# A token-routing kernel: a third copy of the expert slots, whose last slot is 160 columns wide

## The chip, the cores and the metric

The kernel runs on one core of one Trainium2 chip. The metric is device time in microseconds (us): the median of several executions. A profile of one more execution gives the times of single instructions. Engines are called PE (TensorE, matrix multiply), PEld (its weight loads), DVE (VectorE), ACT (ScalarE), POOL (GpSimd) and SP (SyncE, which issues DMAs).

## The reference, cut to what matters

Three stages follow each other: a linear attention over 4 x 768 positions, a mixture of eight experts in which each of the 3072 tokens goes to one expert, and a dense max-out layer.

```python
def _moe_ref(x, modality_id, w_gate, modality_bias, w1, w2):   # x: 3072 x 384
    logits = x @ w_gate + modality_bias[modality_id]           # 8 experts
    e_idx = np.argmax(logits, axis=1)
    ...
    for e in range(E):
        mask = e_idx == e
        h = np.maximum(x[mask] @ w1[e], 0.0)                   # 384 -> 1024
        out[mask] = gate_w[mask, None] * (h @ w2[e])           # 1024 -> 384

def _moe2_ref(x, w1, w2, w3, w_out):
    h = np.maximum(np.maximum(x @ w1, x @ w2), x @ w3)
    return (h @ w_out)
```

How many tokens an expert gets depends on the data. Computed with this reference on its inputs, experts 4, 5 and 6 get 149, 1354 and 1569 tokens and the other five get none.

## The kernel before

The attention runs over 24 tiles of 128 positions. When 16 of them are done, the kernel picks the expert that leads so far (expert 6) and begins to load its weights. The expert stage is cut into slots. A slot gathers the tokens of one expert, at most as many as it has columns, transposes them (`turn`), and runs eight steps `f` over the 1024 hidden features. A step does nine matmuls of the first layer (`first`, L940, three chunks of 128 inputs times three hi/lo products in fp32r, a rounded 4-byte type that the profile prints as f32) and, one step behind, nine of the second layer (`second`, L952). So a slot is 144 matmuls, each with a weight load of 128 columns. ACT and DVE take the hidden values out (`hid`, L943 and L944).

The first three slots are 256 columns wide and all belong to the leading expert. For the rest the kernel chooses one of nine widths, 256 to 384 in steps of 16, on the chip: `Routing.counting` counts the tokens of each expert, works out how many slots each width needs (`per`, `num`), prices them (`cost`) and writes the index of the choice to `sel`. Its work is a chain of small DVE instructions, spread over the steps of slot 0 as a Python generator: `during(f)` asks for the next piece at each step from f = 2 on, so each `yield` puts the rest one step later. The pieces follow the `hid` of their step on DVE. What is left at the end of slot 0 is then issued, and right behind it all five engines load `sel` into a register:

```python
for _ in tally:
    pass
moe.tail = (0, SLOT, still)
chosen = moe.value(route.sel, every, 2 * NW - 1)
```

Only then do slots 1 and 2 follow, with `Routing.placing`, which works out the table of slots (`tab`) on DVE. Behind slot 2 every engine jumps, by the register `chosen`, into one of 18 straight copies of the remaining slots: for each width one that has exactly as many slots as are sure for it, and one that asks after each further slot whether it is there. With the counts above, expert 6 has 801 tokens left after 768, expert 5 has 1354 and expert 4 has 149. At 272 columns that is 3 + 5 + 1 = 9 slots, the cheapest by `cost` and just the sure number, so the exact copy of width 272 runs, slots 3 to 11. Slot 11 is the one slot of expert 4; it takes 272 columns for its 149 tokens. Into these slots the conversion of the max-out weights (L1046 to L1065, on DVE, POOL and SP) and the last part of the routing (`finals`, L552 on PE) are mixed as side jobs. After slot 11 `leave` copies its result to `yt`, and the max-out stage (L1132 and L1157) follows.

Of the kernel before, what the change touches and what calls it, by code (L numbers as in the profile page):

```python
# [16 lines left out]
ALU = mybir.AluOpType  # L17
AX = mybir.AxisListType
# [5 lines left out]
P = 128  # L24
# [4 lines left out]
E = 8  # L29
SLOT = 256  # L30
WIDTHS = tuple(range(SLOT, SLOT + P + 1, P // 8))
NW = len(WIDTHS)
WIDE = WIDTHS[-1]
NJW = (NT - SLOT) // SLOT + 1
OWN = WIDE // P
AHEAD = 3


def last_slot(w):
    return AHEAD + (NT - SLOT - E) // w + E  # L40


def sure_slots(w):
    return AHEAD - (-(NT - AHEAD * SLOT) // w)
# [337 lines left out]
class Routing:  # L382
    def __init__(self, tc, const, ps):
# [18 lines left out]
        self.wsure = const.tile([P, NW], F32, name="wsure")  # L402
        self.wj = const.tile([P, NW, NJW], F32, name="wj")
        self.jj = const.tile([P, NJW], F32, name="jj")
        self.off = const.tile([P, 1, E], F32, name="off")
# [13 lines left out]
    def setup(self):  # L419
# [18 lines left out]
        for i, w in enumerate(WIDTHS):  # L438
            nc.gpsimd.memset(self.wsure[:, i:i + 1], float(sure_slots(w) - AHEAD))
        nc.gpsimd.iota(self.jj, [[1, NJW]], base=0, channel_multiplier=0, **io)  # L440
        yield
        nc.gpsimd.tensor_tensor(self.wj, self.wv.unsqueeze(2).to_broadcast([P, NW, NJW]),
                                self.jj.unsqueeze(1).to_broadcast([P, NW, NJW]), op=ALU.mult)
        yield
# [160 lines left out]
    def counting(self, wk):  # L605
        nc, V = self.nc, self.nc.vector
        tile = lambda shape, nm, dt=F32: wk.tile(shape, dt, tag=f"rt_{nm}", name=f"rt_{nm}")
        some = tile([P, 1, E], "all", BF16)
        self.tally(NTILE, some)
        cps = self.bank("cps")  # L610
        yield
        cnt = self.counts(wk, NTILE, some, cps)
        row = cnt.rearrange("p e o -> p o e")
        rem = tile([P, 1, E], "rem")
        V.tensor_tensor(rem, row, self.off, op=ALU.subtract)
        key = tile([P, 1, E], "key")
        V.scalar_tensor_tensor(key, row, float(E), self.prio, op0=ALU.mult, op1=ALU.add)
        over = tile([P, NW, E, NJW], "over", F16)
        for i in range(NW):
            V.tensor_tensor(over[:, i], rem[:, 0, :].unsqueeze(2).to_broadcast([P, E, NJW]),  # L620
                            self.wj[:, i:i + 1, :].to_broadcast([P, E, NJW]), op=ALU.is_gt)
            if i in (2, NW - 1):
                yield
        per = tile([P, NW, E], "per")
        V.tensor_reduce(per, over, axis=AX.X, op=ALU.add)
        num = tile([P, NW], "num")
        V.tensor_reduce(num, per, axis=AX.X, op=ALU.add)
        cost = tile([P, NW], "cost")
        V.tensor_tensor(cost, num, self.wcost, op=ALU.mult)
        yield  # L630
        V.tensor_tensor(cost, cost, self.wsel, op=ALU.add)
        least = tile([P, 1], "least")
        V.tensor_reduce(least, cost, axis=AX.X, op=ALU.min)
        pick = tile([P, NW], "pick")
        V.tensor_scalar(pick, cost, least, None, op0=ALU.is_equal)
        V.tensor_tensor(num, num, self.wsure, op=ALU.is_gt)
        V.scalar_tensor_tensor(num, self.wsel, 2.0, num, op0=ALU.mult, op1=ALU.add)
        V.tensor_tensor(num, num, pick, op=ALU.mult)
        V.tensor_reduce(least, num, axis=AX.X, op=ALU.add)
        V.tensor_copy(self.sel, least[0:1])  # L640
        self.plan = row, key, per, pick
        yield
# [169 lines left out]
class Experts:  # L812
# [5 lines left out]
    def open(self, st):  # L818
        tc = self.tc
        pool = st.enter_context(tc.tile_pool(name="mx", bufs=1))  # L820
        self.xg = [[pool.tile([P, DM], F32, name=f"xg{i}_{a}") for a in range(2)] for i in range(2)]
        self.xh, self.xl = ([pool.tile([P, KC, WIDE], F32R, name=f"{q}0")] for q in ("xh", "xl"))
        self.raw = (pool.tile([P, KC, FF], F32, name="raw1"), pool.tile([P, KF, DM], F32, name="raw2"))
        self.w = {nm: pool.tile(shape, F32R, name=f"w_{nm}")
                  for nm, shape in (("h1", [P, KC, FF]), ("l1", [P, KC, FF]), ("h2", [P, KF, DM]), ("l2", [P, KF, DM]))}
        self.hid = pool.tile([P, 4 * WIDE], F32R, name="hid")

# [47 lines left out]

    def gather(self, k, n=WIDE):
        for a in range(-(-n // P)):
            self.fetch(k, a, self.rt.gidx[:, OWN * k:OWN * (k + 1)])
# [31 lines left out]
    def open_more(self, pool):  # L910
        for i in range(2):
            self.xg[i] += [pool.tile([P, DM], F32, name=f"xg{i}_{a}") for a in range(2, OWN)]
        self.xh.append(pool.tile([P, KC, WIDE], F32R, name="xh1"))
        self.xl.append(pool.tile([P, KC, WIDE], F32R, name="xl1"))

# [79 lines left out]
        if job is not None:  # L995
            job(f)

    def slot(self, k, n, stop, total, side=()):
        r = self.regs(k, stop)
        sure = sure_slots(n)  # L1000

        def when(i, what):
            if i < min(sure, stop):
                what()
            elif i < stop:
                with self.tc.If(total > i):
                    what()

        cum = [len(side) * c // 18 for c in (0, 3, 6, 9, 12, 15, 17, 18, 18)]
        for f in range(KF):  # L1010
            if f == KF - 1:
                when(k + 1, lambda: self.turn(k + 1, n))
            self.step(k, f, n, r)
            if f == 0:
                when(k + 2, lambda: self.gather(k + 2, n))
            for j in side[cum[f]:cum[f + 1]]:
                j()
        self.tail = (k, n, r)
# [178 lines left out]
def build(tc, aps):  # L1197
    nc = tc.nc
    ET = mybir.EngineType
    with ExitStack() as st:  # L1200
# [4 lines left out]
        with tc.manual_schedule(), ExitStack() as right, ExitStack() as left:  # L1205
            att = Attention(tc, aps, const, ps, dram, x_dram)
            moe = Experts(tc, aps, att.ident, ps, x_dram)
# [4 lines left out]
            route = moe.rt = Routing(tc, const, ps)  # L1212
            mo = MaxOut(tc, aps, route, ps)
            side = route.setup()
            every = (ET.PE, ET.Activation, ET.DVE, ET.Pool, ET.SP)
# [8 lines left out]
            for s in range(NTILE):  # L1224
                att.step(s, hook)
                if s == EARLY + 1:
                    for _ in side:
                        pass
                    side = route.opening(rw, att.logits, att.bias, EARLY, lambda: moe.load_all(
                        moe.value(route.toptab[:, 0:1], (ET.SP,), E - 1)))  # L1230
# [47 lines left out]
            for _ in tally:  # L1278
                pass
            moe.tail = (0, SLOT, still)  # L1280
            chosen = moe.value(route.sel, every, 2 * NW - 1)
            ahead = lambda: tc.switch_hint({e: chosen for e in every}, 2 * NW, "width")
            with tc.If(moe.many > 0) as both:
                places = route.placing(rw)
                for k in range(1, AHEAD):
# [18 lines left out]
            total = moe.tab(0, NSLOT, every, NSLOT)  # L1304
# [7 lines left out]
            conv = mo.converters(left.enter_context(tc.tile_pool(name="m2tmp", bufs=1, reuse_waits="tile")))  # L1312
            jobs, finals = route.landing(mo.land, att.logits)

            for i in tc.Switch({e: chosen for e in every}, 2 * NW, "width"):
                n, exact = WIDTHS[i // 2], i % 2 == 0
                sure = sure_slots(n)
                stop = sure if exact else last_slot(n)
                moe.tail = (AHEAD - 1, SLOT, moe.regs(AHEAD - 1, stop))
                for k in range(AHEAD, sure):  # L1320
                    a, b = (len(conv) * q // (sure - AHEAD) for q in (k - AHEAD, k - AHEAD + 1))
                    c, d = (len(jobs) * q // (sure - AHEAD - 1) for q in (k - AHEAD, k - AHEAD + 1))
                    side = conv[a:b]
                    for q, j in enumerate(jobs[c:d]):
                        side.insert(7 * q + 3, j)
                    if k == sure - 1:
                        for q, j in enumerate(finals):
                            side.insert(3 * q + 1, j)
                    moe.slot(k, n, stop, total, side)
                if exact:  # L1330
                    moe.end()
                    continue

                def more(k):
                    if k == stop:
                        moe.end()
                        return
                    tail = moe.tail
                    with tc.If(total > k) as going:
                        moe.slot(k, n, stop, total)  # L1340
                        more(k + 1)
                    moe.tail = tail
                    with going.Else():
                        moe.end()

                more(sure)
# [55 lines left out]
```

## Time and profile before

| | |
|---|---|
| median of 3 runs | 711.36 us (710.59 to 713.24) |
| the profiled execution | 713.69 us, its span from the first to the last instruction 712.0 us |
| granted TensorE clock, mean | 0.969 of full speed |
| busy PE | 672.2 us, 94% of the span |
| busy DVE, ACT, POOL | 409.7, 230.3, 238.9 us |

The profiled execution took 2.3 us longer than the median. Its stages: the attention up to about 152 us, slots 0 to 2 up to 214 us, slots 3 to 11 from 216 to 402 us, the max-out layer from there on. A start-to-start distance of two matmuls, read off the timeline, is the pace of PE; the busy time of one matmul is longer, because matmuls are pipelined.

### The profile page before, as it was taken

How to read it: one execution, taken by the hardware profiler on the slowest of the kernel's cores; microseconds unless marked ns; L12 is line 12 of the kernel's file. 1: busy time of each engine (PE TensorE's matmuls, PEld its weight loads, DVE VectorE, ACT ScalarE, POOL GpSimd, SP SyncE). 2: the span in 40 equal slices, each digit the busy share in tenths (PEclk: the TensorE clock that was granted, in tenths of full speed). 3: DMA queues.
4: the chain of work that ended last, by engine and by line, in shares of the span. 5: the costliest groups of instructions: out<-in, count | busy, mean ns of one | idle time of the engine just before them, and what ended most of it. 6: DMA issues, size and time to landing. Idle time of an engine off the chain costs nothing.

```text
span 712.0 us, 13675 instructions
## 1 busy us (share of the span) xinstructions
PE 672.2 (94%) x5007; PEld 607.6 (85%) x5007; DVE 409.7 (58%) x849; ACT 230.3 (32%) x545; POOL 238.9 (34%) x257
## 2 busy tenths in 40 slices
PE   7998979898998998999999899999999999999995
PEld 4887868788998998999989788888888888888884
DVE  6999988838845788878787755322322322222321
ACT  3755754552221244222243334111111211211211
POOL 6877764255032338532255201030210220210202
PEclk8999997889999999999999999999999999999999
DMA  8987865620023471322731000010000100100101
GB/s 229 307 244 235 258 203 176 209 73 24 1 62 109 126 223 54 113 85 72 209 105 46 4 0 1 0 45 1 30 15 1 44 1 1 44 1 1 44 1 45
DMA packets 36251, 61.32 MB, mean 86 GB/s; under 512 B 4880, under 2 KB 24976, under 8 KB 36160
## 3 DMA queue, kind: packets, MB, share of 16 engines
q1 hardware_dynamic: 32512, 49.02, 22.9%
q0 software_dynamic: 3648, 11.21, 5.1%
q8 instruction: 42, 0.69, 0.4%
q14 instruction: 49, 0.40, 0.2%
HBM read 50.77 MB, written 9.44 MB: 85 GB/s over the span
## 4 chain that ended last, share of the span: by engine, by line
PE 43%; issue 11%; DVE 2%; POOL 1%; ACT 0%; POOLq 0%; DVEq 0%; ACTq 0%
PE l L1132 24%; PE o L1157 7%; PE acc L952 6%; PE h L940 6%; POOL out_dram L1168 1%; PE inv_out L552 1%; DVE hid L944 0%; PE t L889 0%; DVE m2wo L1062 0%; DVE m2wl L1096 0%; DVE m2raw L1058 0%; POOL x2l L1119 0%; DVE m2wo L1054 0%; PE acc L889 0%; POOLq L1398 0%
## 5 line engine op out<-in xcount | busy, mean ns | idle before, releaser
L1136 DVE TENSOR_TENSOR tm<-tm,l 128x512 f32<-128x512 f32 x72 | 49.4, 687 | 174.2 <-PE l L1132 174.2
L952 PE MATMUL acc<-hid,w_h 128*128 128x272 f32 (+1 forms) x576 | 125.3, 291 | 6.1 <-DVE hid L944 5.6
L1132 PE MATMUL l<-x2h,m2wh 128*128 128x512 f32 x324 | 126.2, 390 | 1.8 <-ACT m2wh L1100 1.8
L1132 PE MATMUL l<-x2h,m2wl 128*128 128x512 f32 x324 | 127.3, 394 | 0.5 <-DVE m2wl L1096 0.5
L1132 PE MATMUL l<-x2l,m2wh 128*128 128x512 f32 x324 | 127.3, 394 | 0.0
L952 PEld LDWEIGHTS acc<-hid,w_h 128*128 128x128 f32 x576 | 96.8, 190 | 8.7 <-DVE hid L944 8.2
L940 PE MATMUL h<-xh,w_h 128*128 128x272 f32 (+1 forms) x288 | 85.2, 296 | 2.8 <-ACTq L1305 1.9
L943 ACT ACTIVATE hid<-h 128x272 fp32r<-128x272 f32 (+1 forms) x96 | 37.8, 394 | 147.5 <-PE h L940 141.1
L940 PE MATMUL h<-xl,w_h 128*128 128x272 f32 (+1 forms) x288 | 83.0, 288 | 0.5 <-DVE xl L892 0.5
L940 PE MATMUL h<-xh,w_l 128*128 128x272 f32 (+1 forms) x288 | 83.1, 289 | 0.3 <-POOL w_l L865 0.3
L952 PE MATMUL acc<-hid,w_l 128*128 128x272 f32 (+1 forms) x288 | 83.0, 288 | 0.0
L1168 POOL DMA_INDIRECT out_dram<-o,row x24 | 23.6, 984 | 160.0 <-ACT o L1165 154.5
L1132 PEld LDWEIGHTS l<-x2h,m2wl 128*128 128x128 f32 x324 | 61.2, 189 | 13.7 <-DVE m2wl L1096 0.9
L1132 PEld LDWEIGHTS l<-x2h,m2wh 128*128 128x128 f32 x324 | 61.0, 188 | 13.8 <-ACT m2wh L1100 2.0
L1132 PEld LDWEIGHTS l<-x2l,m2wh 128*128 128x128 f32 x324 | 61.2, 189 | 12.5 <-DVE x2l L1096 0.5
L1139 ACT CAST hh<-tm 128x512 fp32r<-128x512 f32 x36 | 22.4, 622 | 149.3 <-DVE tm L1136 149.3
L944 DVE SCALAR_TENSOR_TENSOR hid<-h,hid 128x272 fp32r<-128x272 f32 (+1 forms) x96 | 41.5, 432 | 45.0 <-ACT hid L943 40.5
L223 ACT ACTIVATE A<-ident,dot 128x128 f32<-128x128 f32 x192 | 58.7, 391 | 6.9 <-DVE dot L217 6.7
L940 PEld LDWEIGHTS h<-xh,w_h 128*128 128x128 f32 x288 | 55.0, 191 | 3.4 <-issue 3.1
L940 PEld LDWEIGHTS h<-xl,w_h 128*128 128x128 f32 x288 | 54.9, 191 | 0.9 <-DVE xl L892 0.9
L940 PEld LDWEIGHTS h<-xh,w_l 128*128 128x128 f32 x288 | 54.7, 190 | 0.7 <-POOL w_l L865 0.5
L952 PEld LDWEIGHTS acc<-hid,w_l 128*128 128x128 f32 x288 | 54.9, 191 | 0.0
(272 smaller groups left out, 1213.2 us busy)
## 6 DMA issues: line engine op xcount, KB each, us to landing
raw<-in_moe_w_dram SPq DMA_DIRECT2D x24, 384.0 KB, 4.3
m2raw<-in_moe_w_dram SPq DMA_DIRECT2D x18, 384.0 KB, 3.2
kT<-in_kT_dram SPq DMA_DIRECT2D x24, 224.0 KB, 4.1
rT<-in_rT_dram SPq DMA_DIRECT2D x24, 224.0 KB, 4.3
kn<-in_kn_dram SPq DMA_DIRECT2D x24, 192.0 KB, 4.2
rn<-in_rn_dram SPq DMA_DIRECT2D x24, 192.0 KB, 4.5
vn<-in_vn_dram SPq DMA_DIRECT2D x24, 192.0 KB, 4.5
x_rows<-x SPq DMA_DIRECT2D x24, 192.0 KB, 2.7
```

The costliest lines, as they stand in the source:

```text
L223: nc.scalar.mul(t["A"][:, h % 2, h // 2, :], self.ident, t["dot"][:, h:h + 1])
L552: self.nc.tensor.matmul(inv, lhsT=self.lo[:, i, :], rhs=hi[:, :, i], start=(i == 0), stop=(i == n - 1), skip_group_check=True)
L940: nc.tensor.matmul(ps, lhsT=s[w][:, c, fs], rhs=x[:, c, :], start=(i == 0), stop=(i == 3 * KC - 1))
L943: nc.scalar.activation(hh, ps, AF.Relu)
L944: nc.vector.scalar_tensor_tensor(hl, ps, 0.0, hh.bitcast(F32), op0=ALU.max, op1=ALU.subtract)
L952: nc.tensor.matmul(self.bank[c][:, 0:n], lhsT=s[w][:, f, v], rhs=x, start=(f == 0 and q == 0), stop=(f == KF - 1 and q == 2), skip_group_c ...
L1132: nc.tensor.matmul(ps, lhsT=w[:, m, c, fs], rhs=x[:, c, :], start=(n == 0), stop=(n == 3 * KC - 1))
L1136: nc.vector.tensor_tensor(t, t, ps, op=ALU.max)
L1139: nc.scalar.copy(hh, t)
L1157: self.nc.tensor.matmul(self.acc[a], lhsT=x[:, v], rhs=w[:, f, :], start=(f == 0 and q == 0), stop=(f == NF - 1 and q == 2))
L1168: nc.gpsimd.indirect_dma_start(out=self.out[n], out_offset=bass.IndirectOffsetOnAxis(ap=self.rt.row[:, n:n + 1].bitcast(U32), axis=0), in_ ...
```

## The change

`counting` gets a block of fourteen more DVE instructions in place of one. They find the expert that comes last in order, and how many tokens its last slot will hold at each width; where that is at most NARROW = 160, the index is that of a new kind of copy. There are now 27 copies, three for each width. The new kind is the exact one, with a last slot of 160 columns: its transposes (`after`), its matmuls, the hidden values and `leave` have 160 columns, while its gather stays as wide as before. In `counting` a `yield` is added in the middle of the new block.

```diff
+NARROW = SLOT // 2 + 32
...
         V.tensor_scalar(pick, cost, least, None, op0=ALU.is_equal)
         V.tensor_tensor(num, num, self.wsure, op=ALU.is_gt)
-        V.scalar_tensor_tensor(num, self.wsel, 2.0, num, op0=ALU.mult, op1=ALU.add)
+        lk, lm = tile([P, 1, E], "lk"), tile([P, 1], "lm")
+        V.tensor_scalar(lk, rem, 0.0, 1e9, op0=ALU.is_le, op1=ALU.mult)
+        V.tensor_tensor(lk, lk, key, op=ALU.add)
+        V.tensor_reduce(lm, lk, axis=AX.XY, op=ALU.min)
+        V.tensor_scalar(lk, lk, lm, None, op0=ALU.is_equal)
+        yield
+        pl = tile([P, NW, E], "pl")
+        V.tensor_tensor(pl, per, lk.to_broadcast([P, NW, E]), op=ALU.mult)
+        fill = tile([P, NW], "fill")
+        V.tensor_reduce(fill, pl, axis=AX.X, op=ALU.add)
+        V.tensor_scalar(fill, fill, -1.0, None, op0=ALU.add)
+        V.tensor_tensor(fill, fill, self.wv, op=ALU.mult)
+        V.tensor_tensor(lk, lk, rem, op=ALU.mult)
+        V.tensor_reduce(lm, lk, axis=AX.XY, op=ALU.add)
+        V.tensor_scalar(lm, lm, float(NARROW), None, op0=ALU.subtract)
+        V.tensor_scalar(fill, fill, lm, None, op0=ALU.is_lt)
+        V.scalar_tensor_tensor(num, num, 2.0, fill, op0=ALU.mult, op1=ALU.max)
+        V.scalar_tensor_tensor(num, self.wsel, 3.0, num, op0=ALU.mult, op1=ALU.add)
         V.tensor_tensor(num, num, pick, op=ALU.mult)
         V.tensor_reduce(least, num, axis=AX.X, op=ALU.add)
         V.tensor_copy(self.sel, least[0:1])
...
-    def slot(self, k, n, stop, total, side=()):
+    def slot(self, k, n, stop, total, side=(), after=None, sure=0):
         r = self.regs(k, stop)
-        sure = sure_slots(n)
+        after = after or n
...
-                when(k + 1, lambda: self.turn(k + 1, n))
+                when(k + 1, lambda: self.turn(k + 1, after))
...
-            chosen = moe.value(route.sel, every, 2 * NW - 1)
-            ahead = lambda: tc.switch_hint({e: chosen for e in every}, 2 * NW, "width")
+            chosen = moe.value(route.sel, every, 3 * NW - 1)
+            ahead = lambda: tc.switch_hint({e: chosen for e in every}, 3 * NW, "width")
...
-            for i in tc.Switch({e: chosen for e in every}, 2 * NW, "width"):
-                n, exact = WIDTHS[i // 2], i % 2 == 0
+            for i in tc.Switch({e: chosen for e in every}, 3 * NW, "width"):
+                n, exact, last = WIDTHS[i // 3], i % 3 < 2, NARROW if i % 3 == 0 else WIDTHS[i // 3]
...
-                    moe.slot(k, n, stop, total, side)
+                    moe.slot(k, n if k < sure - 1 else last, stop, total, side, last if k == sure - 2 else n, sure)
```

## Rows read from the trace of the kernel before

**Rows 1.** Part 1 of the page: busy us, share of the span, instructions.

```profile
PE 672.2 (94%) x5007; PEld 607.6 (85%) x5007; DVE 409.7 (58%) x849; ACT 230.3 (32%) x545; POOL 238.9 (34%) x257
```

**Rows 2.** Groups by line and shape: count, busy us, mean ns, idle before.

```profile
L940 PE MATMUL h<-xh,w_h 128*128 128x272 f32 x216 | 64.0, 296 | 1.9 <-ACTq L1305 1.9
```

**Rows 3.** PE's timeline, start and duration in us: each pair bounds equal matmuls.

```profile
203.84 0.28 PE L940 MATMUL h<-xh,w_h 128*128 128x256 f32 x1
...
206.00 0.28 PE L940 MATMUL h<-xh,w_h 128*128 128x256 f32 x1
...
310.74 0.29 PE L940 MATMUL h<-xh,w_h 128*128 128x272 f32 x1
...
313.00 0.29 PE L940 MATMUL h<-xh,w_h 128*128 128x272 f32 x1
...
699.99 0.34 PE L1157 MATMUL o<-m2oh,hh 128*128 128x384 f32 x1
...
703.46 0.34 PE L1157 MATMUL o<-m2oh,hl 128*128 128x384 f32 x1
```

**Rows 4.** Single lines: ns minimum, median, maximum; first and last start.

```profile
L952 PEld LDWEIGHTS acc<-hid,w_l x288: 187/188/335, 154.7 to 401.3; 128*128 128x128 f32 x144
...
L248 PEld LDWEIGHTS xps<-A,vn x304: 118/136/231, 41.2 to 150.3; 128*48 128x48 f32 x133, 128*64 128x64 f32 x19
...
L889 PEld LDWEIGHTS t<-ident,xg x72: 137/141/231, 146.8 to 375.1; 128*128 128x128 f32 x72
L889 PE MATMUL t<-ident,xg x72: 270/273/477, 146.8 to 375.2; 128*128 128x128 f32 x72
```

**Rows 5.** PE's timeline: plain f32 matmuls of 120 and transposes of 128 columns.

```profile
82.66 0.50 PE L267 MATMUL xnps<-turn,xT 112*128 112x120 f32 x3
...
83.33 0.28 PE L267 MATMUL xnps<-turn,xT 112*128 112x120 f32 x1
...
210.32 0.82 PE L889 MATMUL t<-ident,xg 128*128 128x128 f32 x6
```

**Rows 6.** DVE's timeline in step 6 of slot 0.

```profile
170.62 0.41 DVE L944 SCALAR_TENSOR_TENSOR hid<-h,hid 128x256 fp32r<-128x256 f32 x1
170.95 0.16 DVE L631 TENSOR_TENSOR rt_cost<-rt_cost,wsel 128x9 f32<-128x9 f32 x1
...
172.29 0.14 DVE L640 CAST sel<-rt_least 1x1 int32<-1x1 f32 x1
172.36 0.40 DVE L944 SCALAR_TENSOR_TENSOR hid<-h,hid 128x256 fp32r<-128x256 f32 x1
```

**Rows 7.** Instructions on the tile `sel`: PE's sequencer loads it.

```profile
L832 PEldq TENSOR_LOAD <-sel x1: 311/311/311, 172.5 to 172.5; - x1
```

**Rows 8.** PE's timeline around that load; in brackets idle time and releaser.

```profile
171.90 0.28 PE L952 MATMUL acc<-hid,w_h 128*128 128x256 f32 x1
173.00 0.38 PE L940 MATMUL h<-xh,w_h 128*128 128x256 f32 x1 [0.82 <-DVE hid L944]
```

**Rows 9.** PE after its wait for `tab`; then windows: third number from last, granted clock.

```profile
215.93 0.36 PE L940 MATMUL h<-xh,w_h 128*128 128x272 f32 x1 [1.95 <-ACTq L1305]
...
217.00:218.00 1.00, 1.00 (x8) 1.00 (x7) 0.00 (x0) 0.17 (x1) 0.00 (x0) 0.65 0.04 8
218.00:219.00 1.00, 1.00 (x7) 1.00 (x6) 0.44 (x1) 0.50 (x2) 0.13 (x1) 0.50 0.06 16
219.00:220.00 1.00, 1.00 (x7) 1.00 (x7) 0.42 (x1) 0.47 (x2) 0.81 (x1) 0.50 0.50 61
220.00:221.00 1.00, 1.00 (x7) 1.00 (x7) 0.00 (x0) 0.00 (x0) 0.88 (x1) 0.64 0.71 261
```

**Rows 10.** PE after a longer wait, in the attention, and a later window.

```profile
104.93 1.06 PE L255 MATMUL ups<-vn,kw 128*64 128x48 f32 x16 [3.14 <-DVEq L1219]
...
112.00:114.00 2.00, 2.00 (x27) 2.00 (x26) 0.37 (x2) 0.11 (x1) 0.00 (x0) 0.50 0.89 267
```

**Rows 11.** PE's timeline where slot 11 begins.

```profile
375.34 0.49 PE L889 MATMUL acc<-ident,xg 128*128 128x128 f32 x3
...
378.49 0.39 PE L940 MATMUL h<-xl,w_h 128*128 128x272 f32 x1 [0.27 <-DVE xl L892]
```

## The prediction

> **What bounds the kernel now.** I read the page's shares first: PE is busy for 94% of the span [rows 1], so a saving must come off PE's row, and a cost counts where PE stands still. Then the groups by shape: the first expert layer has 216 matmuls of 272 columns with the operand pair xh, w_h, 24 to a slot, so nine slots ran at 272 columns [rows 2]. That is the exact copy of width 272, and its last slot holds the 149 tokens that the reference gives to expert 4. Third, the timeline gives PE's pace. Eighteen starts take 2.16 us at 256 columns and 2.26 us at 272, twenty take 3.47 us at 384 [rows 3]: 120.0, 125.6 and 173.5 ns a matmul. From 256 to 384 that is 0.418 ns a column, one column a cycle of 2.4 GHz, plus some 13 ns. Down to 256 columns the columns set the pace. Last I looked for the places where PE waits on the chain that the change lengthens; there is one, the load of `sel`.
>
> **The narrow slot.** Slot 11 keeps its 144 matmuls and its 144 weight loads; only the columns go from 272 to 160. No fp32r matmul under 256 columns is in this trace, so the pace is bounded from both sides. If the columns go on setting it, it is 120.0 - 96 x 0.418 = 80 ns. But each matmul needs a fresh weight load of 128 columns. Such a load lasts 188 ns, one of 48 or 64 columns 136 ns [rows 4]: 64 to 80 columns less save 52 ns, 0.65 to 0.81 ns each, so by estimate 128 columns occupy the loader for 83 to 104 ns. At 160 columns the stream takes 67 ns, less than that, and the next load, not the columns, should set the pace. The nearest row for a load of 128 four-byte columns behind a short matmul of the whole array is the plain f32 matmul of 120 columns: six starts in 83.33 - 82.66 us, 112 ns [rows 5]. The most it should be on this account is the 120 ns of 256 columns. I take 115 ns: (125.6 - 115) x 144 = 1.5 us saved, between 0.8 (120 ns) and 2.0 (112 ns). A second reading, that columns alone set it, is worth (125.6 - 80) x 144 = 6.6 us and is a rival below.
>
> The transposes of slot 11 need two blocks instead of three. That takes three PE instructions out, at 109 ns each (six in 0.82 us, the last of 273 ns: 0.55 / 5) [rows 4, 5]: 0.3 us. The third block's xl also holds up PE by 0.27 us as slot 11 begins [rows 11]; with two blocks that wait goes, at most another 0.3 us. ACT's and DVE's work on `hid` gets shorter and is hidden behind PE in either kernel. The gather stays as wide, so POOL's queue and its DMAs don't change. Saved in all: 1.5 + 0.3 + 0.3 = 2.1 us.
>
> **The longer chain to `sel`.** Before, the block behind the cost (L631 to L640, eight DVE instructions) starts at 170.95 us and ends with the CAST to `sel` at 172.29 + 0.14 = 172.43 us: seven steps in 1.34 us, 0.191 us each [rows 6]. All of it follows `hid` of step 6; `hid` of step 7 comes behind it at 172.36 us, at once, so it was ready. The change takes one of these instructions out and puts fourteen in, and its `yield` moves thirteen of the resulting twenty-one behind `hid` of step 7. Step by step: eight in step 6, from 170.95 to 170.95 + 8 x 0.191 = 172.48 us; `hid` of step 7, 0.33 us until the next starts (as 170.62 to 170.95) [rows 6], 172.81 us; thirteen more, the last of them the CAST: 172.81 + 12 x 0.191 + 0.14 = 175.24 us. Two of them work on 72 elements, not 9, and may take a little longer. `sel` is there 2.8 us later.
>
> Does something hide this? PE loads `sel` at 172.5 us, as it appears [rows 7], after it has already stood still: its last matmul of slot 0 starts at 171.90, the next one at 173.00 us, 0.57 us behind the CAST, with 0.82 us idle [rows 8]. Behind the load stand all of slot 1's matmuls, so PE has nothing else to do, and neither have ACT (its `hid`), POOL (its gathers) and SP (its weight loads), which load the same register. DVE's later work, `placing`, waits for PE's next `hid` step by step, so it moves along and catches nothing up. The whole 2.8 us falls on PE, which then idles 0.82 + 2.8 = 3.6 us and resumes at about 175.8 us. The lower bound is 2.5 us, should `hid` of step 7 cost the chain nothing; the upper 3.3 us, if reduce and broadcast forms cost 0.04 us more each.
>
> **What the idle time does to the clock.** After 1.95 us of waiting at 215.93 us the granted clock fell to 0.50 (1.2 GHz) between 217 and 221 us although PE was dense by then: 0.65, 0.50, 0.50, 0.64 in four windows of 1 us [rows 9]. The shortfall is 0.35 + 0.50 + 0.50 + 0.36 = 1.7 us. After the 0.82 us at 173 us PE kept the pace. In the attention a wait of 3.14 us left the clock at 0.50 still 7 us later [rows 10], among less dense work. A new wait of 3.6 us is longer than both, so I charge one such fall, 1.7 us; nothing at the least, and 3.5 us, the half of seven, at the most. The larger table of copies is entered by one jump as before; I price it at nothing, as it is off every loop; should the jump be slower, PE's wait of 1.95 us grows by it.
>
> **The sum.** 2.8 + 1.7 - 2.1 = +2.4 us. The profiled execution would go from 713.69 to 716.1 us. It lies 2.3 us above the median, so the median goes from 711.36 to 713.8 us, 0.3% slower. About 0.5%, 3.6 us, is what a measurement of this kernel can tell from no change. With the clock's fall and the bounds of the terms this case reaches from 2.5 + 1.7 - 2.6 = +1.6 to 3.3 + 3.5 - 1.1 = +5.7 us, mostly 713 to 715.5.
>
> **Rivals.**
>
> *The columns set the pace below 256 as well* (15%). For it speaks the straight line through three widths [rows 3], against it the length of the weight loads [rows 4] and the 112 ns at 120 columns [rows 5]. Saved 6.6 + 0.6 = 7.2 us against 4.5: 708.7 us; with no fall of the clock 707.0 us, which is faster by over 0.5%. The Trainium skill bears on this one: "TensorE: Matmul & The Clock Gate", section "Back-to-back issue gap", puts an isolated gap at N/2.4 + 2.5 ns, 69 ns for 160 columns by estimate; by that the slot would give back 144 x (125.6 - 69) = 8.2 us. At 256 columns this trace has 120 ns where the rule gives 109.
>
> *Under 256 columns fp32r falls back to the rate of plain f32* (13%). Plain f32 moves 128 columns in 109 ns in the transposes, although their weight loads are the shorter ones (141 ns) [rows 4, 5]: two cycles a column. At 160 columns that is 136 ns, or 146 with the gap of the fp32r rows. It decides from some 135 to 150 columns up, where two cycles a column, with or without that gap, exceed 125.6 ns. The slot then costs 1.5 to 2.9 us: +4.5 - 0.6 + 1.5 to 2.9, 716.8 to 718.2 us, slower. Nothing in the rows says that fp32r does this; the kernel only has no fp32r matmul below 256. The Trainium skill speaks against the change more strongly: "FP8 and Floating Point Precision", section "TensorE Precision Notes", counts four passes for true FP32. For 160 columns that is an estimated 267 ns and 20 us for the slot; the 109 ns above are two cycles, not four.
>
> *The wait comes but the clock stays up* (12%), as it did after 0.82 us: 2.8 - 2.1 = +0.7, 712.1 us.
>
> *The new copy isn't chosen* (3%), because the index comes out as the full exact copy: only the wait is paid, 715.9 us. By the counts, (1 - 1) x 272 < 149 - 160 is false, so the index is 3 x 1 + 0, the narrow one.
>
> **Chances.** The forecast has 57%; a quarter of it, 14%, lies above +3.6 us (wait and clock at their upper ends). Slower by over 0.5%: 14 + 13 + 3 = 30%. Faster: half of the first rival, 8%. Within 0.5%: 62%. The range reaches to the first rival's 708.7 and to the top of the second's: 708.5 to 718.
>
> **What would show it.** In the new trace: `sel`'s CAST near 175.2 us and PE resuming near 175.8 after 3.6 us idle; a window of granted clock near 0.50 right after; slot 1 then starting 2.8 us late and slot 3 about 4.5 us late. In slot 11: starts of equal matmuls 112 to 120 ns apart (80 and 136 to 146 decide for the rivals), weight loads that still last 188 ns, six transposes and no wait for xl. The prediction fails if `sel` turns out to be needed later than I read it, if the clock stays low for longer than 4 us, or if the pace is outside these bounds.

## The result and the profile after

The changed kernel takes 715.16 us in the median of 12 runs (710.46 to 719.05), the kernel before 710.86 us in 12 runs beside them (708.42 to 717.45). The ratio is 1.0058, 95% interval 1.003 to 1.0085: 0.6% slower, +4.1 us with +2.1 to +6.0. That lies inside the predicted range, 1.4 us above the predicted time and just over the line of 0.5%. Two further comparisons of the same kernel (below) give 0.9995 and 1.0044. The three differences, +4.1, -0.4 (0.0005 x 719.92) and +3.1 us (0.0044 x 711.3), have a mean of +2.3; the forecast was +2.4. Each has an interval of 2 to 3 us to either side, so the medians alone don't show the forecast's size. The execution profiled for e0_third was a slow one, 2% above the fastest of its runs, so only its slots 0 to 2 and 11 are used below.

The profiled execution took 717.7 us, its span 716.0 us, 4.0 us more than before. Part 1 of the page of the changed kernel, which answers to [rows 1]:

```profile
PE 667.7 (93%) x5004; PEld 602.7 (84%) x5004; DVE 414.8 (58%) x861; ACT 229.1 (32%) x544; POOL 237.8 (33%) x257
```

PE has three instructions less (the third block's transposes). DVE has twelve more: thirteen in `counting`, and one less for the third block's `xl`. The groups by shape show that the narrow copy ran: 24 + 24 + 24 + 48 + 24 = 144 matmuls of 160 columns, of which two groups stand here, and beside them the pair of [rows 2], now 192 instead of 216 times at 272 columns:

```profile
L970 PE MATMUL acc<-hid,w_h 128*128 128x160 f32 x48 | 9.2, 276 | 0.0
L958 PE MATMUL h<-xh,w_h 128*128 128x160 f32 x24 | 7.1, 296 | 0.0
L958 PE MATMUL h<-xh,w_h 128*128 128x272 f32 x192 | 56.0, 292 | 1.9 <-ACTq L1323 1.9
```

**The chain to `sel`.** DVE's timeline of the changed kernel, beside [rows 6]; L962 is `hid`, L632 the block's first instruction, L642 the last ahead of the new `yield`, L658 the CAST to `sel`:

```profile
172.10 0.41 DVE L962 SCALAR_TENSOR_TENSOR hid<-h,hid 128x256 fp32r<-128x256 f32 x1
172.43 0.16 DVE L632 TENSOR_TENSOR rt_cost<-rt_cost,wsel 128x9 f32<-128x9 f32 x1
173.64 0.23 DVE L642 TENSOR_SCALAR rt_lk<-rt_lk,rt_lm 128x8 f32<-128x8 f32 x1
173.78 0.42 DVE L962 SCALAR_TENSOR_TENSOR hid<-h,hid 128x256 fp32r<-128x256 f32 x1
174.11 0.22 DVE L645 TENSOR_TENSOR rt_pl<-rt_per,rt_lk 128x72 f32<-128x72 f32 x1
176.58 0.14 DVE L658 CAST sel<-rt_least 1x1 int32<-1x1 f32 x1
```

From the block's start to the end of the CAST it takes 176.72 - 172.43 = 4.29 us, where the forecast counted 170.95 to 175.24, also 4.29. The equality is partly luck: the eight steps ahead of the `yield` took 1.35 us (0.169 us each), the twelve between the first and the last behind it 2.47 us (0.206 each), and 0.191 for all misses the two by 0.18 us in opposite directions. PE loads the value and goes on; its timeline and its sequencer's load, beside [rows 7, 8]:

```profile
L850 PEldq TENSOR_LOAD <-sel x1: 306/306/306, 176.8 to 176.8; - x1
...
173.38 0.28 PE L970 MATMUL acc<-hid,w_h 128*128 128x256 f32 x1
177.29 0.57 PE L958 MATMUL h<-xh,w_h 128*128 128x256 f32 x1 [3.63 <-DVE sel L658]
```

PE starts 0.57 us behind the CAST, as before, and has been idle for 3.63 us instead of 0.82.

**The clock.** Windows of the changed kernel behind that wait, and two behind the wait for `tab`, which answer to [rows 9] (third number from last, the granted clock):

```profile
177.00:178.00 1.00, 0.71 (x3) 0.72 (x4) 0.00 (x0) 0.00 (x0) 0.00 (x0) 0.58 0.00 0
178.00:179.00 1.00, 1.00 (x7) 1.00 (x6) 0.00 (x0) 0.00 (x0) 0.00 (x0) 0.50 0.00 0
179.00:180.00 1.00, 1.00 (x6) 1.00 (x6) 0.00 (x0) 0.34 (x1) 0.00 (x0) 0.50 0.00 0
180.00:181.00 1.00, 1.00 (x8) 0.96 (x8) 0.54 (x2) 0.41 (x2) 0.00 (x0) 0.71 0.00 0
181.00:182.00 1.00, 1.00 (x17) 1.00 (x16) 0.93 (x6) 0.37 (x1) 0.00 (x0) 1.00 0.00 0
...
222.00:223.00 1.00, 0.91 (x5) 0.76 (x6) 0.00 (x0) 0.00 (x0) 0.00 (x0) 1.00 0.06 16
223.00:224.00 1.00, 1.00 (x10) 1.00 (x9) 0.00 (x0) 0.00 (x0) 0.00 (x0) 1.00 0.05 16
```

Right behind the new wait PE runs at 0.50 (1.2 GHz). The counts hold every matmul that touches a window, so also those that cross its edges: 6 to 7 at half clock against 10 at full clock (the 17 of the window from 181 on hold short ones). Summed over the windows of slots 1 and 2, the clock is short of full by 1.64 us. Behind the wait for `tab`, where it fell before, it stays at 1.00; what that was worth is taken up below.

**Slot 11 and the wait for `tab`.** PE's timeline of the changed kernel, beside [rows 3, 5, 9, 11]:

```profile
222.09 0.36 PE L958 MATMUL h<-xh,w_h 128*128 128x272 f32 x1 [1.93 <-ACTq L1323]
229.68 0.52 PE L970 MATMUL acc<-hid,w_h 128*128 128x272 f32 x2 [1.09 <-DVEq L988]
...
381.23 0.82 PE L907 MATMUL t<-ident,xg 128*128 128x128 f32 x6
384.55 0.34 PE L958 MATMUL h<-xl,w_h 128*128 128x160 f32 x1 [0.17 <-DVE xl L910]
...
400.62 0.27 PE L958 MATMUL h<-xh,w_h 128*128 128x160 f32 x1
402.63 0.27 PE L958 MATMUL h<-xh,w_h 128*128 128x160 f32 x1
```

Eighteen starts take 402.63 - 400.62 = 2.01 us: 111.7 ns a matmul at 160 columns, against 125.6 at 272. There are six transposes, not nine, and a wait for `xl` of 0.17 us is left of 0.27. The transposes run ahead of slot 11's first matmul, so what they save shows in slot 10. Its first matmul and that of slot 11, before and after:

```profile
356.57 0.29 PE L940 MATMUL h<-xh,w_h 128*128 128x272 f32 x1
377.93 0.28 PE L940 MATMUL h<-xh,w_h 128*128 128x272 f32 x1
...
363.09 0.29 PE L958 MATMUL h<-xh,w_h 128*128 128x272 f32 x1
384.14 0.24 PE L958 MATMUL h<-xh,w_h 128*128 128x160 f32 x1
```

Slot 10 takes 21.05 us instead of 21.36. In all traces it takes 21.36 to 21.38 us ahead of a wide slot 11 and 21.02 to 21.05 ahead of one with two blocks, that of 224 columns in e5 included.

### The profile page after: what moved, and what is told of

Same layout as the page of the kernel before. It is cut to its first block, busy times and chain, and to the rows that moved or that the text cites. A ratio compares the mean times of both kernels' runs of the same rounds, so it can differ in the third digit from the quotient of the medians.

```text
span 716.0 us, 13680 instructions
## 1 busy us (share of the span) xinstructions
PE 667.7 (93%) x5004; PEld 602.7 (84%) x5004; DVE 414.8 (58%) x861; ACT 229.1 (32%) x544; POOL 237.8 (33%) x257
## 4 chain that ended last, share of the span: by engine, by line
PE 42%; issue 11%; DVE 2%; POOL 1%; ACT 0%; POOLq 0%; DVEq 0%
PE l L1150 23%; PE o L1175 7%; PE acc L970 5%; PE h L958 5%; POOL out_dram L1186 1%; PE inv_out L553 1%; DVE hid L962 0%; PE t L907 0%; DVE m2wo L1080 0%; DVE m2raw L1076 0%; POOL x2l L1137 0%; DVE m2wl L1114 0%; DVE m2wo L1072 0%; PE acc L907 0%; POOLq L1416 0%
## 5 line engine op out<-in xcount | busy, mean ns | idle before, releaser
L970 PE MATMUL acc<-hid,w_h 128*128 128x272 f32 (+2 forms) x576 | 124.3, 289 | 7.4 <-DVE hid L962 5.8
L958 PE MATMUL h<-xh,w_h 128*128 128x272 f32 (+2 forms) x288 | 84.8, 294 | 5.6 <-DVE sel L658 3.6
L961 ACT ACTIVATE hid<-h 128x272 fp32r<-128x272 f32 (+2 forms) x96 | 37.1, 386 | 150.7 <-PE h L958 134.5
L958 PE MATMUL h<-xl,w_h 128*128 128x272 f32 (+2 forms) x288 | 82.8, 288 | 0.4 <-DVE xl L910 0.4
L958 PE MATMUL h<-xh,w_l 128*128 128x272 f32 (+2 forms) x288 | 82.9, 288 | 0.3 <-POOL w_l L883 0.3
L970 PE MATMUL acc<-hid,w_l 128*128 128x272 f32 (+2 forms) x288 | 82.5, 286 | 0.0
L962 DVE SCALAR_TENSOR_TENSOR hid<-h,hid 128x272 fp32r<-128x272 f32 (+2 forms) x96 | 40.6, 423 | 45.3 <-ACT hid L961 40.9
L890 POOL DMA_INDIRECT xg<-x_rows,gidx x33 | 31.7, 962 | 73.4 <-PE h L958 43.8
```

Source lines behind the costliest of these rows:

```text
L890: self.nc.gpsimd.indirect_dma_start(out=self.xg[k % 2][a], out_offset=None, in_=self.x_dram[0:rows, :], in_offset=bass.IndirectOffsetOnAxi ...
L958: nc.tensor.matmul(ps, lhsT=s[w][:, c, fs], rhs=x[:, c, :], start=(i == 0), stop=(i == 3 * KC - 1))
L961: nc.scalar.activation(hh, ps, AF.Relu)
L962: nc.vector.scalar_tensor_tensor(hl, ps, 0.0, hh.bitcast(F32), op0=ALU.max, op1=ALU.subtract)
L970: nc.tensor.matmul(self.bank[c][:, 0:n], lhsT=s[w][:, f, v], rhs=x, start=(f == 0 and q == 0), stop=(f == KF - 1 and q == 2), skip_group_c ...
```

## The stages of every trace

The stages below are differences of starts on PE's timeline: the first matmul of slot 0; the first of slot 3; the first of slot 11; the first of the max-out; the span's end. The span's end is read to 0.1 us. The last column is from slot 0 to the end, so without the attention, whose instructions no kernel here changes.

| trace | slot 0 starts at | slots 0-2 | slots 3-10 | slot 11 | max-out | from slot 0 |
|---|---|---|---|---|---|---|
| before | 152.45 | 63.48 | 162.00 | 25.70 | 308.37 | 559.55 |
| b_again (before, once more) | 152.67 | 63.68 | 162.42 | 25.69 | 307.64 | 559.43 |
| after | 153.94 | 68.15 | 162.05 | 23.42 | 308.44 | 562.06 |
| e0_third (after) | 157.71 | 67.85 | 163.10 | 23.42 | 308.22 | 562.59 |
| e1_wide_b | 153.22 | 69.10 | 162.42 | 25.71 | 309.75 | 566.98 |
| e2_short_chain_b | 156.79 | 63.58 | 162.05 | 23.45 | 307.53 | 556.61 |
| e3_filled_b | 150.30 | 66.29 | 162.08 | 23.40 | 307.93 | 559.70 |
| e4_late_load | 153.03 | 62.93 | 161.94 | 23.41 | 307.79 | 556.07 |
| e5_short_224 | 151.49 | 63.61 | 162.32 | 23.53 | 307.55 | 557.01 |
| e7_late_filled | 145.70 | 63.08 | 162.41 | 23.43 | 307.48 | 556.40 |
| first set: e0_again (after) | 147.68 | 70.43 | 164.62 | 23.42 | 307.95 | 566.42 |
| first set: e1_wide_last | 149.64 | 71.69 | 164.96 | 25.68 | 307.63 | 569.96 |
| first set: e2_short_chain | 151.85 | 66.72 | 164.41 | 23.41 | 308.11 | 562.65 |
| first set: e3_filled_wait | 150.50 | 70.27 | 164.09 | 23.42 | 308.22 | 566.00 |

Of the profile's +4.0 us, 153.94 - 152.45 = 1.5 arose ahead of slot 0. The same kernel (after) shows 147.68, 153.94 and 157.71 us there, so that part isn't the change's. The rest, 562.06 - 559.55 = +2.5 us, stands against the forecast of +2.4. Against b_again, the same kernel before in another execution, it is +2.6.

## The experiments

**Theory.** The change costs the wait for `sel` (2.8 us) and one fall of the clock (1.7), and gives back some 2 us in slot 11, where the weight load, not the columns, sets the pace. **Rivals.** The columns set the pace of the narrow slot; or the loss comes from elsewhere: the larger table of copies, the attention, or the measurement.

### e0_again and e0_third: the changed kernel once more

No edit. The runs came in three sets; e0_again belongs to the first, beside e1_wide_last, e2_short_chain and e3_filled_wait, and e0_third to the third, beside e1_wide_b, e3_filled_b and e7_late_filled.

> The changed kernel once more, on the chip that also runs the three kernels below. Between the two traces so far the stages differ by: attention +1.5 us, from hid of step 6 in slot 0 to the first matmul of slot 1 +2.8, slots 1 and 2 +1.9, slots 3 to 10 +0.05, slot 11 -2.3. My theory: the +2.8 (later load of sel) and the +1.9 (clock after the idle time) come again in every run, the -2.3 too, and the +1.5 of the attention does not belong to the change: +2.4 us, ratio 1.0035. Rival: the attention's +1.5 does belong to it (a longer program): +4 us or more, ratio 1.006.

> The changed kernel a third time, since one of its two traces was taken on a chip whose DVE stood still several times without a releaser. My theory: from the first matmul of slot 0 to that of slot 1 23.35 us (20.55 in the kernel before), from there to slot 3 44.8 (43.0), slot 11 23.4 (25.7), together +2.4 us; a fall of the clock by 1.6 to 1.7 full-speed us behind the load of sel. Rival (the first trace's +1.9 in slots 1 and 2 was chance): 43.0 us there.

Measured: e0_again 720.23 us, ratio 0.9995 (0.9958 to 1.0032), beside a kernel before that took 719.92 us in this set, 9 us above the other sets. e0_third 714.47 us, 1.0044 (1.0006 to 1.0082). All traces of the first set have slots 0 to 2 some 2 to 4 us and slots 3 to 10 some 1.5 to 3 us longer than the same kernel later; lines of e2_short_chain from ACT's and PE's timelines show where:

```profile
212.38 0.38 ACT L944 ACTIVATE hid<-h 128x256 fp32r<-128x256 f32 x1 [5.32 <-issue]
218.57 0.56 PE L941 MATMUL h<-xh,w_h 128*128 128x272 f32 x1 [4.20 <-ACTq L1306]
```

ACT stands 5.32 us for nothing that the profile shows, and PE waits 4.20 us at the start of slot 3 instead of 1.93 to 1.95. The same kernel in the second set hasn't got it (63.58 and 162.05 us), nor has the third set, which ran on the chip of the first; so it belongs to that occasion. What makes ACT stand there stays open.

### e1_wide_last and e1_wide_b: the long chain without the narrow slot

```diff
-n, exact, last = WIDTHS[i // 3], i % 3 < 2, NARROW if i % 3 == 0 else WIDTHS[i // 3]
+n, exact, last = WIDTHS[i // 3], i % 3 < 2, WIDTHS[i // 3]
```

> The new chain to sel and the 27 copies stay, but the third kind of copy has a last slot of full width again. My theory: the wait of 2.8 us and the clock's 1.9 us are paid and slot 11 takes 25.7 us again: +4.7 us against the kernel before, ratio 1.0065, and 2.3 us slower than the changed kernel. Rival (the 160 columns cost time, the chain is hidden): the time of the kernel before.

> The chain and the 27 copies with the full last slot once more. My theory: 23.35 and 44.8 us up to slot 3, slot 11 25.7 us: +4.7 us against the kernel before, ratio 1.0065. Rival (part of the 2.3 us of slot 11 is lost elsewhere): below +3.5 us.

Measured: 721.53 us, 1.0048 (1.0011 to 1.0085), and 719.74 us, 1.0097 (1.0059 to 1.0135). Slot 11 is back at 25.68 and 25.71 us, so the narrow slot is worth 2.26 to 2.29 us there, and 0.3 us more in slot 10. The costs of the chain remain, and in the second trace they are greater than one fall of 1.7 us. Windows of e1_wide_b, whose PE resumes at 176.57 us after the same 3.63 us idle:

```profile
176.00:177.00 1.00, 0.43 (x2) 0.44 (x3) 0.00 (x0) 0.00 (x0) 0.00 (x0) 0.50 0.00 0
177.00:178.00 1.00, 1.00 (x6) 1.00 (x6) 0.00 (x0) 0.00 (x0) 0.00 (x0) 0.50 0.00 0
...
181.00:182.00 1.00, 1.00 (x8) 1.00 (x6) 0.70 (x4) 0.18 (x1) 0.00 (x0) 0.50 0.00 0
182.00:183.00 1.00, 1.00 (x7) 1.00 (x7) 0.00 (x0) 0.00 (x0) 0.00 (x0) 0.63 0.06 16
```

The clock is low for more than 6 us here, short by 3.08 us in slots 1 and 2 against 1.64 in after. From slot 0 on this trace is 7.4 us longer than that of before, against +4.7 expected; 1.4 us of it is this longer fall, and 1.4 us the max-out layer, which no edit touches. The prediction's 3.5 us at the most was thus nearly reached, and its own sign of failing, a clock that stays low for longer than 4 us, came up in this execution, though not in those of the changed kernel.

### e2_short_chain and e2_short_chain_b: the narrow slot without the long chain

The new instructions and their `yield` go; the index is 3 x width + (num > sure). The test of how full the last slot is, is left out.

```diff
-        lk, lm = tile([P, 1, E], "lk"), tile([P, 1], "lm")
-        V.tensor_scalar(lk, rem, 0.0, 1e9, op0=ALU.is_le, op1=ALU.mult)
...
-        V.scalar_tensor_tensor(num, num, 2.0, fill, op0=ALU.mult, op1=ALU.max)
         V.scalar_tensor_tensor(num, self.wsel, 3.0, num, op0=ALU.mult, op1=ALU.add)
```

> The thirteen added DVE instructions and the added yield are taken out again; the index is 3 x width + (number over the sure one), so that an exact width always takes the narrow copy, which fits these inputs alone; it leaves out the test of what the last slot holds. 27 copies as in the changed kernel. My theory: sel comes as early as before, PE waits 0.8 us, no fall of the clock behind it, slot 11 takes 23.4 us: -2.3 us against the kernel before, ratio 0.997. Rival (a longer program costs time in the attention or at the jump): +1.5 - 2.3 = -0.8 us or more, with the attention ending near 154 us.

> The short chain with the narrow last slot once more, as its ratio of 0.993 was better than its stages say. My theory: -2.3 us, ratio 0.997, the difference being noise of the runs of the kernel before. Rival: something beyond slot 11 got faster, ratio 0.993 again.

Measured: 714.0 us, 0.9927 (0.9893 to 0.9961), in the first set; 709.79 us, 0.9986 (0.9947 to 1.0024), in the second. The expected 0.997 lies between the two, and outside the first interval. The second trace says more than the medians: slots 0 to 2 take 63.58 us (before 63.48 and 63.68), slot 11 23.45; from slot 0 on it is 2.8 us shorter than b_again. Without thirteen of the fourteen instructions and the `yield` both the longer wait and the fall behind it are gone, so both come from the chain; and the 27 copies, which this kernel has too, cost nothing that shows.

### e3_filled_wait and e3_filled_b: the wait filled with matmuls

27 matmuls whose result isn't read go ahead of the load of `sel`, so that PE works while DVE does. They also measure the pace at three more widths.

```diff
+            spare = ps.tile([P, 512], F32, tag="N", bufs=1, name="spare")
+            for n in (64, 128, 192):
+                for i in range(9):
+                    nc.tensor.matmul(spare[:, 0:n], lhsT=moe.w["h1"][:, i % KC, 0:P], rhs=moe.xh[0][:, i % KC, 0:n],
+                                     start=True, stop=True)
             chosen = moe.value(route.sel, every, 3 * NW - 1)
```

> The changed kernel, with 27 extra matmuls on PE between slot 0 and the load of sel, nine each of 64, 128 and 192 columns with their own weight loads; nothing reads their result. They take the place of PE's idle time (about 3.0 us if each takes 112 ns). My theory: PE still resumes 0.6 us behind the CAST, so the wait costs its 2.8 us, but the clock stays at full speed in slot 1: 1.9 us faster than the changed kernel up to slot 3; part of it may come back if the clock then falls at the next wait, 44 us later, as it did in the kernel before. Rival (the slower slots 1 and 2 are DVE's or POOL's, not the clock's): no gain there. The pace: if the weight load sets it, all three widths come 108 to 113 ns apart; if the columns set it, 40, 67 and 93 ns apart.

> The filled wait once more, beside the changed kernel. My theory: the stage up to slot 1 stays at 23.35 us, the one from there to slot 3 falls from 44.8 to 43.0 us as the clock does not fall; ratio 0.9975 to the changed kernel. Rival: 44.8 us, then the clock is not what slowed slots 1 and 2.

Measured: 719.61 us, 1.0015 (0.998 to 1.0049), and 711.25 us, 0.9998 (0.9965 to 1.003). PE's timeline of e3_filled_wait:

```profile
170.07 3.16 PE L1302 MATMUL spare<-xh,w_h 128*128 128x64 f32 x27
172.95 0.27 PE L1302 MATMUL spare<-xh,w_h 128*128 128x192 f32 x1
173.86 0.38 PE L958 MATMUL h<-xh,w_h 128*128 128x256 f32 x1 [0.64 <-DVE sel L658]
```

From the first start to the last, at 172.95, there are 26 steps in 2.88 us: 111 ns each, over 64, 128 and 192 columns alike. PE is then idle 0.64 us, and in both traces the clock stays at 1.00 until PE has done its work of slots 1 and 2. In e3_filled_b they take 66.29 us with slot 0, 1.56 us less than in e0_third of the same set and 1.86 less than in after; the fall is gone and the wait, now filled, is still paid. In the first set only 0.16 us came of it (70.27 against 70.43): PE waited 4.2 us at the start of slot 3 in both traces, and in e3_filled_wait 1.26 us more late in slot 2, for ACT's `hid`.

### e5_short_224: the last slot at 224 columns

e2_short_chain with another width:

```diff
-NARROW = SLOT // 2 + 32
+NARROW = 224
```

> As the short chain, but the narrow slot has 224 columns. My theory (below some 240 columns the weight load sets the pace): matmuls of slot 11 come 112 ns apart as with 160 columns, and the time is the same within 0.3 us. Rival (the columns count): 112 + 64 x 0.418 = 139 ns is excluded by the 120 ns of 256, but 117 ns or more would show that the columns still matter, 0.7 us or more.

Measured: 713.8 us, 1.0018 (0.9978 to 1.0057), which can't tell a few tenths of a microsecond. The trace can. Two lines of PE's timeline bound 18 starts:

```profile
394.01 0.28 PE L941 MATMUL h<-xh,w_h 128*128 128x224 f32 x1
396.02 0.27 PE L941 MATMUL h<-xh,w_h 128*128 128x224 f32 x1
```

Again 2.01 us, 111.7 ns, exactly the pace of 160 columns, and slot 11 takes 23.53 us against 23.45. From 64 to 224 columns the columns don't matter; the line of [rows 3] meets this floor at an estimated 236 columns: 256 - (120.0 - 111.7) / 0.418.

### e4_late_load and e7_late_filled: the register loaded later

`ahead`, the hint for the jump, is issued at step 6 of slot 2. It now loads `sel` itself there, and the register for the jump is loaded beside `total`, just before slot 3; at the end of slot 0 no engine loads it. e7 adds 6 and 4 matmuls of 128 columns around these loads, whose result isn't read.

```diff
-            chosen = moe.value(route.sel, every, 3 * NW - 1)
-            ahead = lambda: tc.switch_hint({e: chosen for e in every}, 3 * NW, "width")
+            def ahead():
+                soon = moe.value(route.sel, every, 3 * NW - 1)
+                tc.switch_hint({e: soon for e in every}, 3 * NW, "width")
...
+            chosen = moe.value(route.sel, every, 3 * NW - 1)
             total = moe.tab(0, NSLOT, every, NSLOT)
```

> The changed kernel, with the full chain and the narrow slot, but the engines load sel only where it is used: for the prefetch hint in step 6 of slot 2, and once more beside the load of the number of slots behind slot 2. Nothing of the computation is left out. My theory: neither PE's 0.8 us of before nor the 3.6 us of the change are there, no fall of the clock in slot 1; DVE's added 2.5 us fall into time in which it waited for PE, at worst they lengthen its 1.0 us lead over PE in slot 1; two more loads cost 0.3 to 0.6 us each. Against the kernel before -0.8 - 2.3 + 0.3 to 1.2 us = -1.9 to -2.8, ratio 0.9965; against the changed kernel -5 to -7 us. Rival (the chain costs DVE time that PE needs in slots 1 and 2 anyway): no faster than the changed kernel by more than 2 us.

> The late load of sel, and ten extra matmuls of 128 columns (1.1 us) on PE around the load of the number of slots behind slot 2, whose result nothing reads; they take the place of most of the 1.95 us of PE's idle time there, behind which the clock fell by 1.7 us in seven of the eight traces with a full wait. My theory: no fall at slot 3, slots 3 to 10 take 160.3 instead of 162.0 us, -1.7 against the late load, some -5 us against the kernel before, ratio 0.993. Rival (the extra matmuls delay the jump, or a shorter idle time still lets the clock fall): no gain, or a loss of up to 0.6 us.

Measured: e4 709.11 us, 0.9979 (0.9938 to 1.002); e7 706.26 us, 0.9942 (0.9907 to 0.9977), below 1 by more than its interval, as only e2_short_chain in the first set was, which didn't repeat; e7 was run in one set. PE no longer waits for `sel` as slot 1 begins; in e4 slots 0 to 2 take 62.93 us, 0.55 less than before, and all work from slot 0 on 3.5 us less, 0.6 of it in the max-out layer, which no edit touches. For e7 the same sum is 3.2 us, 0.9 of it there; its ratio is worth 4.1 us (0.0058 x 711.3), and what makes the rest isn't shown. e4 and e7 aren't told apart: e7's extra matmuls were to keep the clock up through the wait for `tab`, and that failed. PE's timeline and windows of e7:

```profile
206.44 0.28 PE L970 MATMUL acc<-hid,w_h 128*128 128x256 f32 x1
207.02 1.41 PE L1329 MATMUL spare<-xh,w_h 128*128 128x128 f32 x10 [0.30 <-DVE rt_ef L755]
208.78 0.36 PE L958 MATMUL h<-xh,w_h 128*128 128x272 f32 x1 [0.35 <-issue]
209.49 0.39 PE L958 MATMUL h<-xh,w_l 128*128 128x272 f32 x1 [0.22 <-DVEq L1336]
...
209.00:210.00 1.00, 0.78 (x6) 0.56 (x6) 0.00 (x0) 0.00 (x0) 0.00 (x0) 1.00 0.12 33
210.00:211.00 1.00, 1.00 (x7) 1.00 (x6) 0.00 (x0) 0.00 (x0) 0.00 (x0) 0.52 0.00 0
```

Three waits of 0.30, 0.35 and 0.22 us take the place of one, and the clock falls all the same, by 1.71 us in sum. Slots 3 to 10 take 162.41 us, not 160.3: the rival came true.

### b_again: the kernel before once more

> The kernel before itself, as one of the kernels, for its trace on this chip and as the measure of the noise: ratio 1.000. The four traces of the last call all show PE standing still for some 4.2 us before slot 3, where the first two traces have 1.95 us, and DVE held up several times with nothing that the profile shows to wait for. My theory: that belongs to the chip, so this trace has it too, and slots 1 and 2 last about 46 us in it. Rival: it comes with the 27 copies; then this trace has 1.95 us and 43 us.

Measured: 712.97 us, 1.0014 (0.9974 to 1.0054) against itself. Two sets of runs of one kernel thus differ by 0.14%, with an interval of 0.4% to either side; that is what the medians above can't tell apart. Its trace has PE waiting 1.93 us before slot 3 and 43.1 us in slots 1 and 2, as the rival had it. The copies aren't the cause for all that: e2_short_chain_b, with its 27 copies, has 1.93 and 43.0 us in the same set.

## Why the prediction was right

**The wait, forecast 2.8 us.** From the first matmul of slot 0 to the first of slot 1 it is 23.35 us in after and 20.55 before: 2.80. Eight and thirteen steps around one `hid` were the right count; their price of 0.191 us was 0.169 for the first and 0.206 for the later ones, and the two errors cancel. Nothing hid the chain: e2 takes the instructions out and has 20.54 us there, and e4, which keeps them and moves the load, has no wait for `sel` on PE.

**The fall of the clock, forecast 1.7 us.** The shortfall is 1.64 us in after, 1.71 in e0_again and e0_third, 0 in e3, where PE works through the wait; slots 1 and 2 take 1.87 us longer in after. The rival in which the clock stays up is out. The size came from one fall behind another wait and isn't fixed: it was 3.08 us in e1_wide_b.

**The narrow slot, forecast 2.1 us, measured 2.6:** 25.70 - 23.42 = 2.28 in slot 11 and 21.36 - 21.05 = 0.3 in slot 10. That is the upper bound of the forecast. Of its terms the pace was mis-sized: 111.7 ns, not 115, so (125.6 - 111.7) x 144 = 2.0 us, not 1.5. The transposes went as counted, 0.3 us. The wait for `xl` didn't go: 0.27 - 0.17 = 0.1 us instead of 0.3. Some 0.2 us of slot 11 have no term.

That the columns aren't the limit is shown by 64, 128, 160, 192 and 224 columns at one pace. That the weight load is, is read from rows: no run here changed the load, and those of slot 11 still last 192 ns, the median of each kind. A fixed cost of every pair of load and matmul is excluded by this line of the kernel before, sixteen matmuls, each with a load of its own of 48 or 64 columns:

```profile
85.46 0.62 PE L255 MATMUL ups<-vn,kw 128*48 128x48 f32 x16
```

That is under 40 ns a pair, where 111 ns would need 1.8 us. They go to two parts of the array by turns, so the line doesn't give the price of a load. The 112 ns that plain f32 took at 120 columns [rows 5] had been the lower bound, and was the better value. The Trainium skill, "TensorE: Matmul & The Clock Gate", section "LDWEIGHTS (loading the stationary operand)", counts a weight load by its columns over 1.2, an estimated 107 ns for 128; the traces have 111 to 112, near to it. In the Trainium skill, the rule for an isolated gap in that page's section "Back-to-back issue gap", 69 ns for 160 columns, isn't what this stream does; the same section says that the rule under-counts for small matmuls, as it has no weight load in it.

**The rivals.** Columns setting the pace (80 ns) and the rate of plain f32 (136 to 146 ns) are both refuted by 111.7. The rule of "FP8 and Floating Point Precision", section "TensorE Precision Notes", in the Trainium skill, with its estimated 267 ns, has no trace in its favour here. The narrow copy was chosen.

**What the prediction didn't see.** Behind the wait for `tab` the clock fell by 1.7 us before [rows 9] and in after not at all, yet slots 3 to 10 take 162.00 and 162.05 us. The 1.09 us of PE at 229.68 us point to why. DVE's timeline of after in slot 3, and the DMA issues of that stretch (the last figure is us from issue to landing):

```profile
228.25 0.43 DVE L1072 TENSOR_SCALAR m2w<-m2raw 128x384 int32<-128x384 int32 x1 [2.11 <-DMA m2raw<-in_moe_w_dram]
228.72 0.56 DVE L1080 SCALAR_TENSOR_TENSOR m2w<-m2raw,m2w 128x384 int32<-128x384 int32 x1
229.20 0.43 DVE L962 SCALAR_TENSOR_TENSOR hid<-h,hid 128x272 fp32r<-128x272 f32 x1
...
m2raw<-in_moe_w_dram SPq DMA_DIRECT2D x1, 384.0 KB, 3.3
```

DVE stands 2.11 us ahead of a side job that waits for the max-out weights, and the `hid` that PE needs next comes behind it on DVE. A PE at full clock arrives early and waits; a PE at half clock arrives in time. Two more lines bear this out: the same wait of DVE in before, where the clock had fallen and PE has no wait behind it, and PE's wait in e3_filled_b, where the clock hadn't fallen either:

```profile
221.80 0.36 DVE L1054 TENSOR_SCALAR m2w<-m2raw 128x384 int32<-128x384 int32 x1 [1.85 <-DMA m2raw<-in_moe_w_dram]
...
224.17 0.52 PE L970 MATMUL acc<-hid,w_h 128*128 128x272 f32 x2 [0.81 <-DVEq L988]
```

Slot 10 depends on the width of slot 11, so slots 3 to 9 are compared: they take 140.6 to 141.4 us with a fall (before, b_again, e1_wide_b, e2_short_chain_b, e4, e5, e7) and 141.00 and 141.03 without one (after, e3_filled_b). So the 1.7 us of lost clock are covered there, and by this reading e7 would have gained nothing even with the clock up. That the DMA is the cause is read from these rows; no kernel was run with it issued earlier.

**The sum.** From slot 0 on the change costs +2.5 us in the trace (2.80 for the wait, 1.87 in slots 1 and 2, 0.36 in slots 3 to 9, -0.3 in slot 10, -2.28 in slot 11, 0.07 behind it) for +2.4 forecast. That the sum came so close is luck in part: the narrow slot gave back 0.5 us more than forecast, and against it stand 0.2 us more for the clock and the 0.36 us, which no term foresaw and which b_again has too (141.06 against 140.64 us). What held is the mechanism, and each term to half a microsecond. The rest of the median's +4.1 us isn't distinguished from the scatter of the attention and of the medians.

## What to carry to other kernels

When work is added to a chain, look for the register load at its end: where all engines load the value and have nothing else to do, each instruction counts in full, and an idle PE can pay again with its clock. Loading the same value where it is used (e4) did at least as well as leaving the new instructions out (e2): slots 0 to 2 took 62.93 and 63.58 us, one trace each. With a fresh load of 128 columns for each matmul, as here, a narrower matmul saves only down to a floor, 111 to 112 ns; below it, fewer matmuls, not fewer columns, are what saves.

## What the runs showed of the hardware that was not expected

- The pace of fp32r matmuls with a fresh 128-column weight load is 111 to 112 ns at 64, 128, 160, 192 and 224 columns alike.
- After the same 3.63 us idle, and the same work, the granted clock was low for some 3.3 us of PE's work in one execution (after) and for some 6.2 us in another (e1_wide_b): 1.64 and 3.08 us short, at half clock.
- A wait of 1.93 to 1.95 us for `tab` was followed by a fall in five executions (before, b_again, e1_wide_b, e2_short_chain_b, e5) and by none in two (after, e3_filled_b); three short waits, 0.87 us in all, were followed by one in e7. The length of the wait alone doesn't decide it, and what does stays open.
- The start of slot 0, behind an attention that is the same in all kernels, scatters from 145.70 to 156.79 us over these traces without e0_third, more than any effect studied here.
